# A two-layer network behind an attention scan: the 399 parts of the first block written in another order

## The chip, the cores and the metric

One core of one Trainium2 chip runs the kernel. The metric is the device time in microseconds (us) from the first to the last instruction of one execution, as the median of several executions. The chip's engines are named as the profile names them: PE (TensorE, matrix products; PEld is its weight load), DVE (VectorE), ACT (ScalarE), POOL (GpSimd) and SP (SyncE, which here only issues DMAs). Each engine runs its own list of instructions strictly in the order in which it is written, and waits at an instruction until the semaphores that it needs have come.

## The reference

```python
def _attn_ref(r, k, v, w, u):              # B=4, H=8, S=768, D=48
    for t in range(S):
        cur = np.einsum('bhd,bhe->bhde', u[None] * kt, vt)
        y[:, :, t] = np.einsum('bhd,bhde->bhe', rt, state + cur)
        state = wt[:, :, :, None] * state + np.einsum('bhd,bhe->bhde', kt, vt)

def _moe_ref(x, w1, w2, w3, w_out):        # 3072 tokens, 384 -> 1024 -> 1024 -> 384
    h = ((x @ w1) * (x @ w2)) @ w3
    return h @ w_out

def _moe2_ref(x, w_in, w_out):             # 384 -> 2048 -> 384
    h = x @ w_in
    return (h - np.tanh(h)) @ w_out
```

The output of the attention is the input x of the first network, whose output is the input of the second. The weights of the networks come as 64-bit floats.

## The kernel before

The sequence is cut into 24 **chunks** of 128 positions, and the tokens into six **blocks** of 512, which is four chunks each. The first network can start on a block when the attention of its four chunks is done. w3 and w_out are multiplied into one matrix W first (the **folds**), since nothing stands between them.

The change touches the first block only. There everything has to be prepared for the first time, and it is written out by hand as a list, `ORDER`, of 399 short names; each name is a part of the work and a number. The list is carried out as it stands, and each engine gets its instructions in the order in which the parts give them. The names that matter:

- **Attention of chunk n.** `LPn`, `LKn` load its five tensors (SP). `Dan`, `Dbn` are two scans on DVE, `Drn` a small step on POOL between them, `Dkn` and `Dcn` element-wise products (DVE for chunks 0 to 3, POOL from chunk 4). On PE stand `Sdn` (a diagonal term, chunks 0 to 3; tile psd), `San` (scores, tile psA), `Stn` (transposes, psk), `Sun` (state update, psu), `On` (outputs, psy) and `Wn` (for the first four chunks: a small product that puts 16 rows in their place, psy again). ACT copies out of PSUM (`Sen`, `Sbn`, `SBn`, `Skn`, `Vn`, `Xn`), POOL masks (`Smn`, `SMn`), DVE ends with `Tn` (state) and `Yn` (the rest of x).
- **Weights.** Each piece of 64-bit weights goes through four parts: `lw` fetches it into one of three buffers named st (SP, line 146), `wa` and `wb` take it apart (ACT, lines 168 and 174), and `wj` joins the halves (DVE, two passes, lines 178 and 180). The letter behind says which weight: `a` for the first layer (w1 and w2 together, eight pieces of 768 columns), `o` for w_out (four pieces of 768), `x` and `y` for the two halves of w3 (eight of each, 512 columns). A first-layer piece is then rounded (`wha`, ACT) and its rest taken (`wsa`, DVE, line 202).
- **Fold f** (`Ff`, PE, line 486, tile psW): 8 products of 128x384 that need all of w_out and both halves f of w3. `Faf` (ACT) and `Fdf` (DVE, line 202) write W.
- **First network, piece f of 8.** `Pf` is the product with w1 and w2 (PE, 18 matmuls, tiles psa and psb, lines 206 to 208), `Gaf`, `Gmf`, `Gbf`, `Gsf` the gate (ACT, DVE, ACT, DVE), `Qf` the product with W (PE, 9 matmuls, tile acc). All of `P` needs x of the four chunks.

The three buffers st are reused in turn, so a fetch waits until the piece three places before it has been joined on DVE. SP, too, works in order: a load behind a waiting fetch waits with it. Chunks 4 to 7, which belong to the next block, are prepared inside the list as well, between the products.

After the list the kernel goes on with `pair` (line 780 on), two pieces of the first network and one chunk at a time, and then with the second network. None of that is touched.

Of the kernel before, what the change touches and what calls it, by code (L numbers as in the profile page):

```python
# [40 lines left out]


ORDER = """
LP0 LK0 lwa3 lwa1 lwa2 Da0 LP1 Dr0 K0 Db0 LK1 Dk0 Sd0 Dc0 waa3 wba3 Sa0 Se0 wja3 waa1 Sf0 wba1 St0 lwy3 Sb0 wja1 Sk0
Sm0 SB0 Su0 waa2 SM0 Da1 lwa0 wha3 O0 T0 Dr1 wba2 U0 Db1 LP2 wha1 LK2 V0 Dk1 W0 wsa3 Sd1 X0 Dc1 way3 Se1 wby3 Sf1 Y0
Sa1 wsa1 St1 SB1 Da2 Sb1 SM1 Sk1 wja2 Sm1 waa0 Su1 Dr2 O1 T1 wba0 lwo0 Dk2 U1 Db2 wha2 LP3 Sd2 V1 LK3 wsa2 W1 Se2 Dc2
Sf2 X1 wao0 Y1 Sa2 wja0 St2 Sb2 SB2 Sm2 Da3 lwo1 Sk2 SM2 wbo0 Su2 Dk3 Dr3 wha0 O2 T2 Db3 U2 LP4 wsa0 Sd3 V2 LK4 Dc3
wao1 W2 Se3 X2 wjo0 Sa3 Sf3 SB3 Da4 lwo2 Sb3 St3 SM3 wbo1 Y2 Sm3 Sk3 wjy3 Dr4 O3 Db4 lwo3 wao2 wjo1 Dc4 Su3 LK5 LN4 V3
wbo2 W3 T3 X3 lwa4 wjo2 wao3 U3 Sa4 LP5 wbo3 Y3 lwy0 P0 Sb4 wjo3 SB4 Sm4 Dt4 lwx0 SM4 waa4 De4 St4 LN5 P1 C4 Ga0 Sk4
wba4 Da5 way0 wby0 wja4 Dr5 O4 wax0 Ga1 Dt5 Db5 lwa5 wbx0 Su4 LK6 X4 P2 V4 wha4 T4 Dc5 Gm0 wsa4 Gb0 wjx0 waa5 U4 W4  # L50
lwx2 Sa5 LP6 wjy0 Ga2 wba5 P3 Gm2 lwy2 Sb5 wja5 Gb2 Sm5 SB5 wax2 SM5 Gs2 lwx3 wha5 Y4 wbx2 F0 Da6 Ga3 De5 Dr6 Gm3 LN6
Db6 Gb3 Gs3 Dc6 wsa5 P4 Fa0 Gm1 way2 Fd0 Gb1 Dt6 wjx2 wby2 wax3 Gs1 lwa6 wbx3 wjy2 Sa6 Ga4 P5 wjx3 lwy4 Sb6 SB6 Sm6
De6 lwx1 SM6 Gm4 LN7 waa6 C5 Gb4 F3 wba6 C6 Ga5 Gs4 Dt7 wja6 Gm5 wha6 lwx4 St6 Gs0 F2 Fa3 wsa6 wax1 Sk6 Fd3 wbx1 way4
wjx1 wby4 lwy1 wjy4 Su6 Fa2 O5 wax4 lwx5 Fd2 wbx4 wjx4 Q0 way1 LP7 LK7 V5 X5 T6 lwa7 W5 wby1 U6 Y5 F4 Gb5 wjy1 Gs5
lwx7 LP8 Da7 De7 Dr7 Db7 LN8 F1 Fa4 wax5 Fd4 Dc7 waa7 wbx5 wax7 wjx5 wba7 Da8 lwy6 wbx7 Sa7 Dt8 Fa1 wja7 O6 Sb7 SB7
St7 LK8 V6 Sm7 Fd1 X6 lwy7 Sk7 wjx7 Q1 SM7 way6 Dr8 W6 wha7 lwy5 C7 P6 wby6 wsa7 Y6 wjy6 way7 wby7 Q2 De8 lwx6 Ga6
wjy7 LN9 Su7 Gm6 F7 T7 Gb6 Db8 U7 LP9 Gs6 Dc8 O7 Fa7 way5 Fd7 wax6 Q3 LK9 wby5 X7 wjy5 wbx6 P7 V7 wjx6 W7 Y7 Z7 Q4 Ga7
Gm7 Gb7 F5 Gs7 F6 Fa5 Fd5 Q5 Fa6 Fd6 Q6 Q7
""".split()


# [978 lines left out]
```

## Time and profile before

| what | value |
|---|---|
| median of 3 runs | 907.2 us (905.99 to 907.22) |
| the profiled execution, its own time | 908.82 us |
| its span, first to last instruction | 907.1 us |
| mean granted PE clock | 0.982 |
| PE busy in the span | 861.9 us (95%) |
| DVE, ACT, POOL busy | 614.3, 483.0, 227.3 us |
| DMA | 93.31 MB, mean 103 GB/s |

The profile says for each instruction when it ran and what ended the idle time of its engine before it. The time of the profiled execution lies 1.7 us over its span, and 1.6 us over the median of the three runs. The granted clock is the share of full speed that PE was given: its two levels are 1.2 and 2.4 GHz, shown as 0.5 and 1.0.

### The profile page before, as it was taken

How to read it: one execution, taken by the hardware profiler on the slowest of the kernel's cores; microseconds unless marked ns; L12 is line 12 of the kernel's file. 1: busy time of each engine (PE TensorE's matmuls, PEld its weight loads, DVE VectorE, ACT ScalarE, POOL GpSimd, SP SyncE). 2: the span in 40 equal slices, each digit the busy share in tenths (PEclk: the TensorE clock that was granted, in tenths of full speed). 3: DMA queues.
4: the chain of work that ended last, by engine and by line, in shares of the span. 5: the costliest groups of instructions: out<-in, count | busy, mean ns of one | idle time of the engine just before them, and what ended most of it. 6: DMA issues, size and time to landing. Idle time of an engine off the chain costs nothing.

```text
span 907.1 us, 12892 instructions
## 1 busy us (share of the span) xinstructions
PE 861.9 (95%) x4762; PEld 690.8 (76%) x4762; DVE 614.3 (68%) x884; ACT 483.0 (53%) x879; POOL 227.3 (25%) x223
## 2 busy tenths in 40 slices
PE   5879999999999999799999899999999999999996
PEld 4766767778777777577888688888888888888885
DVE  6889884365666666665567977667667577586763
ACT  4546652123223224422467766596696786786662
POOL 4356241053344543435226310010010010000000
PEclk9789999999999999899999999999999999999999
DMA  8586574134443364631253020220220310300001
GB/s 287 196 273 201 168 262 129 47 111 129 116 154 109 96 242 134 215 117 53 54 180 134 21 61 1 68 72 0 71 69 1 94 47 1 106 23 0 36 1 38
DMA packets 51623, 93.31 MB, mean 103 GB/s; under 512 B 5152, under 2 KB 22688, under 8 KB 51552
## 3 DMA queue, kind: packets, MB, share of 16 engines
q1 hardware_dynamic: 51552, 92.41, 32.2%
q8 instruction: 39, 0.64, 0.3%
q14 instruction: 32, 0.26, 0.1%
HBM read 80.99 MB, written 9.44 MB: 100 GB/s over the span
## 4 chain that ended last, share of the span: by engine, by line
PE 49%; issue 3%; POOL 2%; DVE 1%; DMA 1%; ACT 1%; SPq 0%; ACTq 0%; POOLq 0%
PE acc L206 8%; PE acc L208 8%; PE acc L207 8%; PE psh L206 7%; PE psh L208 7%; PE psh L207 7%; POOL w L202 1%; DMA st<-w 1%; PE psa L206 1%; PE psa L207 1%; PE psa L208 1%; PE psb L207 1%; PE psb L206 1%; PE psb L208 1%; PE psy L395 0%
## 5 line engine op out<-in xcount | busy, mean ns | idle before, releaser
L516 DVE TENSOR_TENSOR g<-psh,g 128x512 fp32r<-128x512 f32 (+1 forms) x99 | 66.4, 672 | 55.3 <-ACT g L515 55.0
L206 PE MATMUL psh<-xt,w 128*128 128x512 f32 x252 | 98.1, 389 | 0.5 <-DVE g L516 0.5
L208 PE MATMUL psh<-xt,w 128*128 128x512 f32 x252 | 98.0, 389 | 0.0
L207 PE MATMUL psh<-xt,w 128*128 128x512 f32 x252 | 98.0, 389 | 0.0
L206 PE MATMUL acc<-g,w 128*128 128x512 f32 x252 | 98.0, 389 | 0.0
L207 PE MATMUL acc<-g,w 128*128 128x512 f32 x252 | 98.0, 389 | 0.0
L208 PE MATMUL acc<-g,w 128*128 128x512 f32 x252 | 98.0, 389 | 0.0
L515 ACT CAST g<-psh 128x512 fp32r<-128x512 f32 (+1 forms) x99 | 56.3, 570 | 63.0 <-DVE psh L582 63.0
L512 POOL TENSOR_TENSOR xt<-x2l,xt 128x512 fp32r<-128x512 f32 x18 | 24.4, 1366 | 258.4 <-ACT xt L511 258.3
L580 DVE TENSOR_TENSOR psh<-psh,z 128x512 f32<-128x512 f32 (+1 forms) x99 | 67.2, 679 | 27.0 <-ACT z L577 26.7
L581 DVE SCALAR_TENSOR_TENSOR psh<-s,psh 128x512 f32<-128x512 f32 (+1 forms) x99 | 67.1, 678 | 19.0 <-ACT s L578 12.6
L577 ACT ACTIVATE z<-psh 128x512 f32<-128x512 f32 (+1 forms) x99 | 57.6, 582 | 30.9 <-PE psh L208 29.3
L582 DVE SCALAR_TENSOR_TENSOR psh<-s,psh 128x512 f32<-128x512 f32 (+1 forms) x99 | 67.2, 679 | 9.5
L578 ACT ACTIVATE s<-z,qa 128x512 f32<-128x512 f32 (+1 forms) x99 | 70.5, 712 | 2.4
L579 ACT ACTIVATE s<-z,qa 128x512 f32<-128x512 f32 (+1 forms) x99 | 69.0, 697 | 0.0
L515 ACT CAST g<-psb 128x512 fp32r<-128x512 f32 x40 | 23.4, 585 | 84.9 <-DVE psb L843 48.8
L206 PE MATMUL psa<-xt,w 128*128 128x512 f32 x144 | 61.8, 429 | 6.9 <-DMA xt<-y 3.3
L337 POOL TENSOR_SCALAR_AFFINE_SELECT A<-A 128x512 f32<-128x512 f32 x48 | 37.6, 804 | 90.9 <-ACT A L332 90.7
L206 PE MATMUL psb<-xt,w 128*128 128x512 f32 x144 | 56.9, 395 | 2.5 <-ACT a L531 2.2
L208 PE MATMUL acc<-g,W 128*128 128x512 f32 x144 | 56.3, 391 | 2.2 <-DVE W L202 2.2
L206 PE MATMUL acc<-g,W 128*128 128x512 f32 x144 | 57.8, 401 | 0.0
L207 PE MATMUL psa<-xt,w 128*128 128x512 f32 x144 | 57.6, 400 | 0.0
(141 smaller groups left out, 1984.0 us busy)
## 6 DMA issues: line engine op xcount, KB each, us to landing
st<-w SPq DMA_DIRECT2D x24, 768.0 KB, 4.4
st<-w3F SPq DMA_DIRECT2D x16, 512.0 KB, 4.7
P<-wP SPq DMA_DIRECT2D x24, 258.0 KB, 2.8
ws<-wS SPq DMA_DIRECT2D x24, 256.0 KB, 3.4
kd<-kT SPq DMA_DIRECT2D x24, 256.0 KB, 3.8
rd<-rT SPq DMA_DIRECT2D x24, 256.0 KB, 4.0
vn<-vN SPq DMA_DIRECT2D x24, 256.0 KB, 3.6
wb<-wP SPq DMA_DIRECT2D x24, 256.0 KB, 3.4
```

Source lines behind the costliest of these rows:

```text
L206: nc.tensor.matmul(ps, lhs(0), rhs(1), start=start, stop=False)
L207: nc.tensor.matmul(ps, lhs(0), rhs(0), start=False, stop=False)
L208: nc.tensor.matmul(ps, lhs(1), rhs(0), start=False, stop=stop)
L337: nc.gpsimd.affine_select(out=A, in_=A, pattern=[[0, NP], [1, C]], compare_op=ALU.is_gt, fill=0.0, base=0, channel_multiplier=-1)
L515: nc.scalar.copy(t[:, 0, :], x)
L516: nc.vector.tensor_sub(t[:, 1, :], x, t[:, 0, :].bitcast(F32))
L577: nc.scalar.activation(out=z, in_=p, func=AF.Square)
L578: nc.scalar.activation(out=s1, in_=z, func=AF.Square, scale=QS, bias=qa[:, 0:1])
L579: nc.scalar.activation(out=s2, in_=z, func=AF.Square, scale=QS, bias=qa[:, 1:2])
L580: nc.vector.tensor_mul(p, p, z)
L581: nc.vector.scalar_tensor_tensor(out=p, in0=s1, scalar=QB1, in1=p, op0=ALU.add, op1=ALU.mult)
L582: nc.vector.scalar_tensor_tensor(out=p, in0=s2, scalar=QB2, in1=p, op0=ALU.add, op1=ALU.mult)
```

## The change

The same 399 parts stand in another order. Three things move. All four pieces of w_out and the halves of w3 are fetched and joined from the start, where three first-layer pieces stood. Folds 0 to 4 stand among the parts of chunks 2 and 3 and fold 5 behind the scores of chunk 4, all ahead of the first product P0; before, fold 0 stood behind four of the products and folds 5 and 6 near the end of the list. The first-layer pieces 0 to 7 are fetched and joined behind that, in the order of their use. No part is added or left out. The first two and the last two lines of the list, before and after:

```diff
-LP0 LK0 lwa3 lwa1 lwa2 Da0 LP1 Dr0 K0 Db0 LK1 Dk0 Sd0 Dc0 waa3 wba3 Sa0 Se0 wja3 waa1 Sf0 wba1 St0 lwy3 Sb0 wja1 Sk0
-Sm0 SB0 Su0 waa2 SM0 Da1 lwa0 wha3 O0 T0 Dr1 wba2 U0 Db1 LP2 wha1 LK2 V0 Dk1 W0 wsa3 Sd1 X0 Dc1 way3 Se1 wby3 Sf1 Y0
...
-wjy7 LN9 Su7 Gm6 F7 T7 Gb6 Db8 U7 LP9 Gs6 Dc8 O7 Fa7 way5 Fd7 wax6 Q3 LK9 wby5 X7 wjy5 wbx6 P7 V7 wjx6 W7 Y7 Z7 Q4 Ga7
-Gm7 Gb7 F5 Gs7 F6 Fa5 Fd5 Q5 Fa6 Fd6 Q6 Q7
+LP0 LK0 lwo0 lwo1 lwx0 Da0 LP1 Dr0 K0 Db0 LK1 Dk0 Sd0 Dc0 wao0 wbo0 Sa0 Se0 wjo0 wao1 Sf0 wbo1 St0 wax0 wjo1 lwy0 Sb0
+SB0 Sm0 Sk0 wbx0 SM0 Su0 Da1 lwo2 O0 Dk1 Dr1 T0 way0 Db1 U0 LP2 wby0 wjx0 Sd1 wao2 LK2 V0 Dc1 lwo3 Se1 W0 wbo2 Sf1
...
+Y6 SB7 Sm7 wsa7 Gb5 St7 SM7 Q3 Gs5 Sk7 Da8 Su7 C7 Dr8 P6 T7 Db8 U7 LP9 De8 Dc8 LN9 O7 Ga6 Gm6 Gb6 Q4 LK9 V7 Gs6 X7 W7
+Y7 P7 Z7 Q5 Ga7 Gm7 Gb7 Q6 Gs7 Q7
```

On PE, from the diagonal term and the placing (`Sd2`, `W1`) at the end of chunk 1's work to the transposes of chunk 2. A w with a number is a half of w3, so two rows of psW are one fold:

```order
 L309 MATMUL psd<-ub,rk 128x2 x4
 L414 MATMUL psy<-y_148 128x128 x3
+L486 MATMUL psW<-wo,w_202 128x384 x4
+L486 MATMUL psW<-wo,w_254 128x384 x4
+L486 MATMUL psW<-wo,w_378 128x384 x4
+L486 MATMUL psW<-wo,w_400 128x384 x4
 L327 MATMUL psA<-rd,kd 128x128 x8
+L486 MATMUL psW<-wo,w_452 128x384 x4
+L486 MATMUL psW<-wo,w_444 128x384 x4
 L349 MATMUL psk<-ident,kd 128x128 x4
-L362 MATMUL psu<-vn,ks 64x48 x8
```

Two folds now stand ahead of chunk 2's scores (psA) and one between its scores and its transposes; the state update (psu) has gone behind the outputs.

On DVE, from the last piece of w_out to the first rest of a fold, after the change (cm into wo is a join of w_out, cm into w_ a join of a half of w3, W the rest of fold 0):

```order
L178 SCALAR_TENSOR_TENSOR cm<-cm,cl 128x768
L180 SCALAR_TENSOR_TENSOR wo<-st,cm 128x768
L289 RECIPROCAL ends<-R 128x64
L292 SCALAR_TENSOR_TENSOR ws<-ws,ends 128x512
L434 TENSOR_TENSOR xt<-psy,xt 128x3x128
L178 SCALAR_TENSOR_TENSOR cm<-cm,cl 128x512
L180 SCALAR_TENSOR_TENSOR w_378<-st,cm 128x512
L178 SCALAR_TENSOR_TENSOR cm<-cm,cl 128x512
L180 SCALAR_TENSOR_TENSOR w_400<-st,cm 128x512
L302 TENSOR_TENSOR rd<-rd,P 128x512
L303 TENSOR_TENSOR kd<-kd,ws 128x512
L202 TENSOR_TENSOR W<-psW,W 128x384
```

Before, the same stretch of chunk 2 held a first-layer piece instead:

```order
L289 RECIPROCAL ends<-R 128x64
L292 SCALAR_TENSOR_TENSOR ws<-ws,ends 128x512
L202 TENSOR_TENSOR w_2_367<-cm,w_2_367 128x768
L302 TENSOR_TENSOR rd<-rd,P 128x512
L303 TENSOR_TENSOR kd<-kd,ws 128x512
L434 TENSOR_TENSOR xt<-psy,xt 128x3x128
L178 SCALAR_TENSOR_TENSOR cm<-cm,cl 128x768
L180 SCALAR_TENSOR_TENSOR cm<-st,cm 128x768
```

So the products rd and kd, which chunk 2's scores need, now stand behind the two halves for fold 1.

On ACT, around `V0`, the copy of 16 rows of chunk 0's output (y_148), first before and then after the change:

```order
L199 CAST w_3_228<-cm 128x768
L174 ACTIVATE cl<-st,qa 128x768
L199 CAST w_1_258<-cm 128x768
L409 COPY y_148<-psy 128x128
L430 CAST xt<-psy 128x3x128
```

```order
L174 ACTIVATE cl<-st,qa 128x512
L168 ACTIVATE cm,tops<-st 128x512
L174 ACTIVATE cl<-st,qa 128x512
L168 ACTIVATE cm,tops<-st 128x768
L409 COPY y_148<-psy 128x128
```

The copy now stands behind the first step (cm) of a piece of 768 columns, the third of w_out, whose fetch must have landed.

## Rows read from the trace of the kernel before

**Rows 1.** The page: PE's busy time in the span; its granted clock in 40 slices

```profile
PE 861.9 (95%) x4762; PEld 690.8 (76%) x4762; DVE 614.3 (68%) x884; ACT 483.0 (53%) x879; POOL 227.3 (25%) x223
...
PEclk9789999999999999899999999999999999999999
```

**Rows 2.** Windows: stretch, length, busy time of each engine, PE's clock, DMA

```profile
8.58:36.28 27.70, 23.44 (x189) 20.54 (x189) 22.01 (x26) 16.48 (x31) 10.16 (x13) 0.82 0.78 269
36.28:89.14 52.86, 43.66 (x362) 35.04 (x361) 47.47 (x55) 29.20 (x56) 30.32 (x28) 0.90 0.69 229
89.14:174.90 85.76, 83.51 (x433) 57.95 (x432) 53.98 (x79) 36.03 (x76) 21.05 (x19) 1.00 0.48 151
```

**Rows 3.** Waits of PE from 36.28 to 89.14 us, longest first

```profile
PE psk L349 <- DVE xt L434: 3.4, 1, 3.4
```

**Rows 4.** Windows of 2 us, PE alone: length, busy time, clock, DMA

```profile
50.00:52.00 2.00, 1.35 (x8) 0.50 0.77 310
52.00:54.00 2.00, 2.00 (x20) 0.50 0.57 144
54.00:56.00 2.00, 2.00 (x38) 0.86 0.96 386
...
78.00:80.00 2.00, 2.00 (x14) 0.61 0.43 121
80.00:82.00 2.00, 2.00 (x7) 0.54 0.89 291
```

**Rows 5.** Groups of PE from 89.14 to 174.9 us by shape: count, busy, mean ns, idle

```profile
L208 PE MATMUL acc<-g,W 128*128 128x512 f32 x24 | 9.5, 396 | 2.2 <-DVE W L202 2.2
```

**Rows 6.** Timeline of PE: start, duration; chunk 1's scores, chunk 2, a fold

```profile
24.14 2.50 PE L327 MATMUL psA<-rd,kd 48*128 48x128 f32 x16 [1.06 <-issue]
...
35.44 0.91 PE L414 MATMUL psy<-y 128*128 128x128 f32 x6
36.28 1.16 PE L327 MATMUL psA<-rd,kd 48*128 48x128 f32 x16
...
39.27 0.67 PE L362 MATMUL psu<-vn,ks 128*64 128x48 f32 x16 [1.11 <-ACT ks L354]
...
43.70 0.91 PE L414 MATMUL psy<-y 128*128 128x128 f32 x6
...
98.93 5.32 PE L486 MATMUL psW<-wo,w 128*128 128x384 f32 x16
104.08 0.60 PE L349 MATMUL psk<-ident,kd 128*128 128x128 f32 x4
```

**Rows 7.** Groups of DVE from 0 to 175 us by shape: count, busy, mean ns

```profile
L178 DVE SCALAR_TENSOR_TENSOR cm<-cm,cl 128x512 int32<-128x512 int32 x16 | 12.8, 801 | 6.4 <-ACT cl L174 6.4
L178 DVE SCALAR_TENSOR_TENSOR cm<-cm,cl 128x768 int32<-128x768 int32 x12 | 12.8, 1063 | 3.2 <-ACT cd L312 2.9 <-ACT cl L174 0.2
L292 DVE TENSOR_TENSOR_SCAN ws<-ws,ends 128x512 f32<-128x512 f32 x9 | 12.6, 1399 | 0.3
L180 DVE SCALAR_TENSOR_TENSOR w<-st,cm 128x512 int32<-128x512 int32 x16 | 12.3, 768 | 1.1
...
L180 DVE SCALAR_TENSOR_TENSOR cm<-st,cm 128x768 int32<-128x768 int32 x8 | 10.1, 1266 | 0.3
L202 DVE TENSOR_TENSOR w<-cm,w 128x768 fp32r<-128x768 f32 x8 | 8.7, 1086 | 0.0
```

**Rows 8.** Timeline of DVE: the last product of chunk 2; one pass of a join

```profile
33.56 0.69 DVE L303 TENSOR_TENSOR kd<-kd,ws 128x512 f32<-128x512 f32 x1
...
74.52 1.67 DVE L178 SCALAR_TENSOR_TENSOR cm<-cm,cl 128x512 int32<-128x512 int32 x1
```

**Rows 9.** DMA issues up to 100 us: count, size, median us from issue to landing

```profile
st<-w3F SPq DMA_DIRECT2D x8, 512.0 KB, 5.4
st<-wo SPq DMA_DIRECT2D x4, 768.0 KB, 4.4
```

**Rows 10.** Timeline of ACT: the copy of 16 rows of chunk 0's output

```profile
20.78 0.27 ACT L409 COPY y<-psy 128x128 f32<-128x128 f32 x1 [1.55 <-PE psy L401]
```

More of the change, by code (lines that the diff above doesn't have):

```diff
@@ L43 @@
 ORDER = """
-LP0 LK0 lwa3 lwa1 lwa2 Da0 LP1 Dr0 K0 Db0 LK1 Dk0 Sd0 Dc0 waa3 wba3 Sa0 Se0 wja3 waa1 Sf0 wba1 St0 lwy3 Sb0 wja1 Sk0
-Sm0 SB0 Su0 waa2 SM0 Da1 lwa0 wha3 O0 T0 Dr1 wba2 U0 Db1 LP2 wha1 LK2 V0 Dk1 W0 wsa3 Sd1 X0 Dc1 way3 Se1 wby3 Sf1 Y0
-Sa1 wsa1 St1 SB1 Da2 Sb1 SM1 Sk1 wja2 Sm1 waa0 Su1 Dr2 O1 T1 wba0 lwo0 Dk2 U1 Db2 wha2 LP3 Sd2 V1 LK3 wsa2 W1 Se2 Dc2
-Sf2 X1 wao0 Y1 Sa2 wja0 St2 Sb2 SB2 Sm2 Da3 lwo1 Sk2 SM2 wbo0 Su2 Dk3 Dr3 wha0 O2 T2 Db3 U2 LP4 wsa0 Sd3 V2 LK4 Dc3
-wao1 W2 Se3 X2 wjo0 Sa3 Sf3 SB3 Da4 lwo2 Sb3 St3 SM3 wbo1 Y2 Sm3 Sk3 wjy3 Dr4 O3 Db4 lwo3 wao2 wjo1 Dc4 Su3 LK5 LN4 V3
@@ L49 @@
[L49 to L53, printed above, removed]
@@ L54 @@
-wjx1 wby4 lwy1 wjy4 Su6 Fa2 O5 wax4 lwx5 Fd2 wbx4 wjx4 Q0 way1 LP7 LK7 V5 X5 T6 lwa7 W5 wby1 U6 Y5 F4 Gb5 wjy1 Gs5
-lwx7 LP8 Da7 De7 Dr7 Db7 LN8 F1 Fa4 wax5 Fd4 Dc7 waa7 wbx5 wax7 wjx5 wba7 Da8 lwy6 wbx7 Sa7 Dt8 Fa1 wja7 O6 Sb7 SB7
-St7 LK8 V6 Sm7 Fd1 X6 lwy7 Sk7 wjx7 Q1 SM7 way6 Dr8 W6 wha7 lwy5 C7 P6 wby6 wsa7 Y6 wjy6 way7 wby7 Q2 De8 lwx6 Ga6
-wjy7 LN9 Su7 Gm6 F7 T7 Gb6 Db8 U7 LP9 Gs6 Dc8 O7 Fa7 way5 Fd7 wax6 Q3 LK9 wby5 X7 wjy5 wbx6 P7 V7 wjx6 W7 Y7 Z7 Q4 Ga7
-Gm7 Gb7 F5 Gs7 F6 Fa5 Fd5 Q5 Fa6 Fd6 Q6 Q7
+LP0 LK0 lwo0 lwo1 lwx0 Da0 LP1 Dr0 K0 Db0 LK1 Dk0 Sd0 Dc0 wao0 wbo0 Sa0 Se0 wjo0 wao1 Sf0 wbo1 St0 wax0 wjo1 lwy0 Sb0
@@ new lines @@
+SB0 Sm0 Sk0 wbx0 SM0 Su0 Da1 lwo2 O0 Dk1 Dr1 T0 way0 Db1 U0 LP2 wby0 wjx0 Sd1 wao2 LK2 V0 Dc1 lwo3 Se1 W0 wbo2 Sf1
+wjy0 X0 Sa1 Sb1 Y0 lwx1 SB1 wjo2 St1 Sm1 Sk1 SM1 Su1 O1 wao3 T1 lwy1 Da2 U1 LP3 wbo3 Dk2 Dr2 wax1 wjo3 Sd2 LK3 V1 wbx1
+W1 way1 X1 Db2 F0 lwy2 wby1 Se2 Sf2 Y1 wjx1 wjy1 lwx2 Fa0 Dc2 F1 lwx3 way2 Fd0 wby2 Dk3 wax2 wjy2 wbx2 wjx2 lwy3 Sa2
+Fa1 Da3 lwx4 wax3 F2 Sb2 Fd1 Dr3 SB2 Sm2 Db3 wbx3 SM2 way3 wjx3 wby3 wjy3 lwy4 St2 wax4 O2 Sk2 Dc3 lwa0 wbx4 Fa2 wjx4
+way4 Su2 LK4 V2 Fd2 lwx5 Sd3 wby4 T2 U2 W2 wjy4 Se3 waa0 Sf3 Sa3 LP4 X2 lwy5 F3 Sb3 Y2 SB3 Sm3 wba0 SM3 wja0 Da4 wha0
@@ new lines @@
+lwa1 St3 Fa3 O3 wsa0 Dr4 Sk3 wax5 Fd3 way5 Db4 wbx5 Su3 LN4 LK5 V3 F4 wby5 T3 Dc4 wjx5 waa1 wjy5 wba1 lwx6 U3 wja1
+lwy6 Dt4 LP5 W3 Fa4 Sa4 X3 Fd4 lwx7 wha1 Y3 F5 De4 wax6 wsa1 LN5 Sb4 SB4 Sm4 wbx6 SM4 Da5 way6 wby6 wjx6 Dr5 St4 Fa5
+Dt5 P0 C4 wax7 lwy7 Sk4 wbx7 wjy6 Fd5 lwa2 wjx7 way7 Su4 Ga0 O4 wby7 T4 lwa3 Gm0 U4 wjy7 Gb0 LP6 F6 V4 LK6 X4 waa2 Gs0
+lwa4 W4 Db5 wba2 waa3 Y4 Dc5 wba3 wja2 P1 Fa6 Fd6 wha2 lwa5 De5 wsa2 LN6 wja3 Sa5 Ga1 waa4 F7 Sb5 Gm1 lwa6 SB5 Sm5 Da6
+Gb1 wha3 SM5 Gs1 wba4 Dr6 wsa3 Dt6 waa5 C5 P2 waa6 wja4 Fa7 wba5 Fd7 wha4 lwa7 De6 O5 wba6 wsa4 LN7 Ga2 Db6 P3 V5 LP7
@@ L59 @@
+LK7 X5 W5 Dc6 Gm2 waa7 Y5 Gb2 wja5 P4 Ga3 Dt7 Gs2 wha5 Gm3 wba7 wsa5 Gb3 Da7 Sa6 Ga4 Gs3 Dr7 Q0 Gm4 Sb6 SB6 De7 Sm6
+Gb4 Db7 LN8 SM6 St6 Q1 Sk6 Gs4 Dc7 C6 Su6 P5 wja6 Dt8 T6 wha6 wja7 U6 O6 LP8 Ga5 Sa7 V6 LK8 wsa6 X6 wha7 Q2 W6 Gm5 Sb7
+Y6 SB7 Sm7 wsa7 Gb5 St7 SM7 Q3 Gs5 Sk7 Da8 Su7 C7 Dr8 P6 T7 Db8 U7 LP9 De8 Dc8 LN9 O7 Ga6 Gm6 Gb6 Q4 LK9 V7 Gs6 X7 W7
+Y7 P7 Z7 Q5 Ga7 Gm7 Gb7 Q6 Gs7 Q7
 """.split()
```

## The prediction

> **What bounds the kernel now.** I read the page first. PE is busy for 95% of the span, and its clock stands at 9 in nearly every slice; the slices below that lie in the first tenth [rows 1]. So time can be won only where PE idles or runs at half clock, and the change can reach only the first block, whose last product ends at 174.9 us. I therefore cut that block into stages. Up to 36.28 us (end of chunk 1 on PE) PE is busy 23.4 of 27.7 us at a mean clock of 0.82; from there to 89.14 us it is busy 43.7 of 52.9 us at 0.90; in the last 85.8 us it is busy 83.5 us at 1.00 [rows 2]. DVE is the other loaded engine: 47.5 us of the middle stage, but only 54.0 of 85.8 us in the last one [rows 2].
>
> The waits of PE in the middle stage tell why. The longest, 3.4 us, is for DVE, which was still joining weights while the transposes of chunk 3 stood at the head of PE's list [rows 3]. PE has nothing else to do there: each chunk's attention is a chain through five engines, and the first product needs x of all four chunks. In the last stage the only wait of size is 2.2 us, for the rest of a fold that stands late in the order [rows 5].
>
> What PE loses after 36.28 us, in three terms:
> - idle in the middle stage: 52.86 - 43.66 = 9.2 us [rows 2];
> - half clock: busy time times (1 - clock), over the five windows where the clock is clearly below 1: 0.68 + 1.00 + 0.28 + 0.78 + 0.92 = 3.7 us [rows 4]. The first three follow the idle of 3.4 us [rows 3];
> - idle in the last stage: 85.76 - 83.51 = 2.2 us [rows 2, 5].
>
> Together 15.1 us. That is the most that the change can win after 36.28 us, since no work is added or taken away.
>
> **What moves.** Six of the eight folds now stand ahead of P0. One fold takes 104.08 - 98.93 = 5.15 us on PE [rows 6], so 31 us of work that needs nothing from the attention is put into a stage that had 9.2 us idle. The order excerpt shows the place: F0 and F1 stand directly behind W1, so PE has work from 36.3 us on without a break, if the folds are fed. P0 comes much later than before, and that costs nothing by itself: the products and folds are all work of the same list, and only idle time counts.
>
> **Are the folds fed?** A fold needs joins on DVE, so I count DVE up to the last join of F0. Before, DVE finished kd of chunk 2 at 33.56 + 0.69 = 34.2 us [rows 8]. After, the same stretch holds four joins of w_out for three of the first layer (one more, 1.06 + 1.27 = 2.3 us), two joins of w3 (2 x 1.57 = 3.1 us) and none of three rests (3 x 1.09 = 3.3 us) [rows 7]; scan, reciprocal and two products of chunk 2 come later (1.4 [rows 7], twice 0.69 [rows 8], and about 0.5 as my estimate for the reciprocal: 3.3 us). So 34.2 + 2.3 + 3.1 - 3.3 - 3.3 = 33.0 us, and PE arrives at 35.44 + 0.84 = 36.28 us [rows 6]: 3 us to spare. F1: scan and reciprocal 1.9 us, then DVE waits for x of chunk 1 (W1 is done at 36.3, ready on DVE at about 37.3 after a copy and a subtraction of half a microsecond each, an estimate), then two joins of 3.1 us: 40.4 us. F0 ends at 36.3 + 5.2 = 41.5 us: 1 us to spare. F2: kd by 41.8, the rest of F0 at 42.5 (it waits for F0), one product 0.7, two joins 3.1: 46.3 us, against 36.3 + 10.4 + 1.2 = 47.9 us on PE: 1.6 us to spare. After that PE falls further behind DVE, since each chunk adds 7.2 us of attention to PE (36.28 to 44.61 less the wait of 1.11 [rows 6]) besides its folds.
>
> The fetches: three buffers st, 5.4 us from issue to landing for a half of w3 [rows 9]. With two steps on ACT and the join, a buffer comes round in about 5.4 + 1.4 + 1.6 = 8.4 us (the ACT share is an estimate), so a fold's two halves every 5.6 us. PE takes 31 us of folds and 16 us of attention from 36.3 us to P0, so a fold every 8 us. That is enough.
>
> The first-layer pieces now come behind the folds. P0 starts at about 36.3 + 31 + 16 = 83 us. DVE has then some 63 us of work left in the block: of 123.5 us busy between 8.58 and 174.9 us [rows 2] its new list has, counted with the means of rows like [rows 7], 60 us up to the rest of the second piece (an estimate). PE has about 79 us left, so the joins (2.3 us) and rests (1.1 us) of a piece lie beside products. Without that cover each late piece would cost up to 3.4 us.
>
> **What is added as waits.** V0 now stands behind a step on the third piece of w_out. Before it ran at 20.78 us [rows 10]. That fetch can be issued when the second join frees its buffer (about 18 us) and lands 4.4 us later [rows 9], so V0 runs at about 23.3 us. Behind it on ACT wait W0's copy and the scores' copies, on PE W0 and Sa1. Sa1 started only at 24.14 us, after a wait of 1.06 [rows 6], so I charge 0.4 us. Two more changes between fold and product on PE cost a few tenths: 0.3 us. And PE will not be gapless: its best long stage before still lost 2.25 of 85.76 us, 2.6% [rows 2], so I charge 2.6% of the 124 us from 36.3 us to the end of the block, 3.2 us.
>
> **Sum.** 15.1 - 0.4 - 0.3 - 3.2 = 11.2 us. The profiled execution took 908.8 us, 1.7 more than its span, so it would take 897.6; it lies 1.6 us over the median of the runs shown, which gives 896.0 us for the median. The first block then ends near 164 us.
>
> **A rule that speaks against it.** One pass of a join of a half of w3 took 1.67 us at 74.5 us [rows 8], while the mean of such passes is 0.77 to 0.80 [rows 7]. The Trainium skill (SBUF — State Buffer, section "Who interferes with whom") says that a DVE instruction with two SBUF inputs and a GpSimd instruction that reads SBUF exclude each other, and the later one blocks for the whole instruction. The long pass agrees with such a block. By the mean the sum stands as above; with every join at the blocked price it is the second rival below.
>
> **Rivals.**
> - *Half of it comes.* Folds F1 and F2 have 1 to 1.6 us to spare by sums of means. If joins slip by 2 to 3 us, PE idles at each, with the clock falling after it as it did behind the 3.4 us wait [rows 3, 4]: two or three times 1 to 2 us. The time is 898.5 to 902. Nothing in the rows excludes it. 0.2.
> - *Slower: the joins meet POOL.* Ten joins of w3 now lie in the stage in which POOL masks and multiplies for chunks 1 to 4 (30.3 us busy before [rows 2]). At 1.67 [rows 8] instead of 0.78 [rows 7] a pass, 20 passes cost DVE 18 us more. It starts with 1 to 2 us to spare, so PE would wait some 16 us and the attention behind the folds with it: 5 us slower, 912. It decides from about 0.65 us more per pass. Against it: the means [rows 7] contain the blocked passes already. 0.08.
> - *No change.* PE's idle time comes back later: pieces 2 to 7 of the first layer arrive late because DVE, in order, waits at each gate for its product and joins the next piece only then. Six pieces at 1.9 us would use up the gain: 906 to 908. DVE's 63 us in PE's 79 us speak against it. 0.08.
> - *More.* The new order loses next to nothing: 15.1 us won, 892 us. 0.04.
>
> The forecast itself, 893.5 to 898.5 us, gets 0.6. A measurement of this kernel tells about 0.2% (1.8 us) from no change. The range reaches from 893 to 902.5 us, the forecast with the first rival, so that about 0.2 is left outside. Faster: 0.6 + 0.2 + 0.04 = 0.84; within 0.2%: 0.08; slower: 0.08.
>
> **What would show it.** In the changed kernel's profile: folds in a row from about 36.5 us; PE busy over 50 of the 52.9 us from 36.3 to 89.1 us, at a clock near 1.0; no wait of PE for a join or a rest (lines 178 to 202) over 1 us; P0 at about 83 us; the last acc product of the block near 164 us; and the time behind it as before. It is wrong if psW products wait for DVE (first rival, or the second if the joins take 1.6 us a pass), or if psa products wait for the rest of a first-layer piece (third).

## The result, and the profile after

The changed kernel took 897.26 us (median of six runs, 896.06 to 901.52); the kernel before took 907.21 us on the same chip (six runs, 905.99 to 912.52). The ratio is 0.9889, with a 95% interval of 0.9859 to 0.9920: 10.1 us faster (7.3 to 12.8). 11.2 us were predicted. The profiled execution of after took 896.06 us, with a span of 894.4 us; it was the fastest of its six.

The page of after, PE's row and its granted clock, beside [rows 1]:

```profile
PE 857.5 (96%) x4762; PEld 686.8 (77%) x4762; DVE 619.8 (69%) x884; ACT 483.7 (54%) x879; POOL 223.1 (25%) x223
...
PEclk9999999999999999899999999999999999999999
```

The windows of after by stage; the first two stretches are those of [rows 2], the third ends at 164 us, where the prediction put the end of the first block:

```profile
8.58:36.28 27.70, 20.63 (x190) 18.17 (x191) 21.92 (x28) 17.56 (x36) 10.57 (x13) 0.94 0.81 281
36.28:89.14 52.86, 52.86 (x373) 36.79 (x372) 46.99 (x59) 31.98 (x68) 17.75 (x19) 1.00 0.68 235
89.14:164.00 74.86, 73.31 (x431) 55.32 (x430) 61.31 (x78) 33.87 (x62) 29.24 (x27) 1.00 0.52 173
```

In the middle stage PE is busy all of the 52.86 us, at a clock of 1.00, where it was busy 43.66 us at 0.90. From 36.28 to 170 us PE waits twice, 1.6 us together:

```profile
PE psA L327 <- DVE Sb L368: 0.9, 1, 0.9
PE psk L349 <- DVE xt L434: 0.7, 1, 0.7
```

The timeline of PE in after, at the place of [rows 6], shows what fills the stage: two folds in one run behind the placing of chunk 1's 16 rows (line 414), a third behind the scores of chunk 2, and so on up to the first product (line 206):

```profile
35.12 0.91 PE L414 MATMUL psy<-y 128*128 128x128 f32 x6
35.87 10.49 PE L486 MATMUL psW<-wo,w 128*128 128x384 f32 x32
46.29 1.16 PE L327 MATMUL psA<-rd,kd 48*128 48x128 f32 x16
47.38 5.43 PE L486 MATMUL psW<-wo,w 128*128 128x384 f32 x16
...
75.67 5.43 PE L486 MATMUL psW<-wo,w 128*128 128x384 f32 x16
80.94 0.60 PE L349 MATMUL psk<-ident,kd 128*128 128x128 f32 x4
81.29 0.48 PE L206 MATMUL psa<-xt,w 128*128 128x512 f32 x1
```

The last product of the first block ended at 160.1 us (175.0 before). A place that both orders pass in the same way lies a little later, the scores of chunk 9. In the timeline of PE before, and then after:

```profile
186.67 1.16 PE L327 MATMUL psA<-rd,kd 48*128 48x128 f32 x16 [1.03 <-POOL kd L303]
```

```profile
173.23 1.16 PE L327 MATMUL psA<-rd,kd 48*128 48x128 f32 x16 [1.00 <-POOL kd L303]
```

The lead there is 13.4 us; the spans differ by 12.7. From these scores to the end of the span all the profiled kernels, those of the experiments too, took between 719 and 722 us: 720.4 before and 721.2 after. So the whole gain lies ahead of this place.

### The profile page after: what moved, and what is told of

It reads as the page before. It is cut to its first block, busy times and chain, and to the rows that moved or that the text cites. A ratio compares the mean times of both kernels' runs of the same rounds, so it can differ in the third digit from the quotient of the medians.

```text
span 894.4 us, 12900 instructions
## 1 busy us (share of the span) xinstructions
PE 857.5 (96%) x4762; PEld 686.8 (77%) x4762; DVE 619.8 (69%) x884; ACT 483.7 (54%) x879; POOL 223.1 (25%) x223
## 4 chain that ended last, share of the span: by engine, by line
PE 50%; issue 3%; POOL 2%; DVE 2%; DMA 1%; ACT 1%; SPq 0%; ACTq 0%; POOLq 0%
PE acc L206 8%; PE acc L208 8%; PE acc L207 8%; PE psh L206 7%; PE psh L208 7%; PE psh L207 7%; POOL w L202 1%; DMA st<-w 1%; PE psa L206 1%; PE psa L208 1%; PE psa L207 1%; PE psb L206 1%; PE psb L208 1%; PE psb L207 1%; PE psy L395 0%
## 5 line engine op out<-in xcount | busy, mean ns | idle before, releaser
L581 DVE SCALAR_TENSOR_TENSOR psh<-s,psh 128x512 f32<-128x512 f32 (+1 forms) x99 | 67.1, 678 | 19.1 <-ACT s L578 12.7
L206 PE MATMUL psa<-xt,w 128*128 128x512 f32 x144 | 61.8, 429 | 4.9 <-DMA xt<-y 3.0
L206 PE MATMUL psb<-xt,w 128*128 128x512 f32 x144 | 57.5, 399 | 2.7 <-ACT a L531 2.7
L206 PE MATMUL acc<-g,W 128*128 128x512 f32 x144 | 58.1, 404 | 0.0
L208 PE MATMUL psa<-xt,w 128*128 128x512 f32 x144 | 57.7, 401 | 0.0
L207 PE MATMUL psa<-xt,w 128*128 128x512 f32 x144 | 57.5, 399 | 0.0
L207 PE MATMUL psb<-xt,w 128*128 128x512 f32 x144 | 56.9, 395 | 0.0
```

Source lines behind the costliest of these rows:

```text
L206: nc.tensor.matmul(ps, lhs(0), rhs(1), start=start, stop=False)
L207: nc.tensor.matmul(ps, lhs(0), rhs(0), start=False, stop=False)
L208: nc.tensor.matmul(ps, lhs(1), rhs(0), start=False, stop=stop)
L581: nc.vector.scalar_tensor_tensor(out=p, in0=s1, scalar=QB1, in1=p, op0=ALU.add, op1=ALU.mult)
```

## The experiments

**Is it the folds ahead of P0?** Two kernels take the folds back behind P0, six of them or three, and leave the joins where after has them. (`late` names the folds moved; they read the two halves of fold 6, so the work is the same, but W is not the reference's.)

```diff
-W1 way1 X1 Db2 F0 lwy2 wby1 Se2 Sf2 Y1 wjx1 wjy1 lwx2 Fa0 Dc2 F1 lwx3 way2 Fd0
+W1 way1 X1 Db2 lwy2 wby1 Se2 Sf2 Y1 wjx1 wjy1 lwx2 Dc2 lwx3 way2
...
-wja2 P1 Fa6 Fd6
+wja2 P1 F3 Fa6 Fa2 Fd6 Fd2
...
+        h = 6 if f in late else f
-                psW[f][:, :DM], w3t[f][m // (NF // 2)]
+                psW[f][:, :DM], w3t[h][m // (NF // 2)]
```

> The changed order, but folds 0 to 5 (with their roundings and rests) moved from chunks 2 to 4 to behind the product P0, between the products; all joins stay where they are. Folds 0 to 5 read the two halves of w3 that belong to fold 6, since there are only four buffers for them, so W is not the reference's. Theory (the folds fill PE's idle time in the chunk stage): from 36 us to P0 PE idles again, over 10 us in sum, partly at half clock; P0 comes at 70 to 74 us instead of 81, but 31 us of folds stand behind it; the last acc product of the block at 180 to 184 us instead of 160; 915 to 921 us. Rival (the gain comes from the new order of the joins on DVE and ACT, the first-layer pieces last, and not from where the folds stand): 896 to 900 us.

Measured: 924.71 us (922.39 to 927.14), ratio 1.0171 (1.0125 to 1.0216), slower than before by more than the change had won. Its windows, its longest waits of PE, and its first product:

```profile
36.28:89.14 52.86, 34.03 (x247) 28.12 (x247) 42.27 (x52) 29.08 (x62) 18.68 (x19) 0.68 0.67 224
```

```profile
PE psk L349 <- DVE xt L434: 8.4, 2, 5.4
PE psA L327 <- issue: 5.8, 1, 5.8
```

```profile
79.91 0.78 PE L206 MATMUL psa<-xt,w 128*128 128x512 f32 x1
```

> As the run before, but only folds 3, 4 and 5 moved behind P0 (they read the halves of fold 6); folds 0 to 2 stay in chunk 2. Theory: PE stays busy to about 58 us, then chunk 3 is a bare chain again; P0 at 70 to 72 us; PE idle of 4 to 6 us and 1 to 2 us of half clock come back: 902 to 905 us. Rival: 896 to 900 us.

Measured: 911.87 us (908.92 to 914.32), ratio 1.0032 (1.0007 to 1.0057).

```profile
36.28:89.14 52.86, 42.93 (x340) 32.35 (x338) 45.79 (x55) 31.12 (x68) 18.87 (x19) 0.87 0.71 232
```

```profile
80.51 0.78 PE L206 MATMUL psa<-xt,w 128*128 128x512 f32 x1
```

The theory holds, and both came out slower than I expected, for one reason. I had let P0 come 7 to 11 us earlier once PE is rid of the folds. It came at 79.9 and 80.5 us instead of 81.3: with the joins of six folds ahead of it on DVE, x of chunk 3 is not ready sooner. So six folds, 31 us of work on PE, put P0 off by only 1.4 us. Counted from the placing of chunk 1's 16 rows, which starts at 35.1 us in after, 36.6 with six and 37.7 with three folds moved back, P0 follows after 46.2, 43.3 and 42.8 us, which makes it about 3 us. Each fold behind P0 costs its full time. From P0 to the last product of the block after takes 160.1 - 81.3 = 78.8 us. With 5.2 us for each fold moved back, 79.9 + 78.8 + 31.2 = 189.9 us and 80.5 + 78.8 + 15.6 = 174.9 us; measured 189.1 and 174.3.

**The wait of 2.2 us in the last stage [rows 5], alone.** In before, the rest of fold 1 is set directly behind its rounding:

```diff
-Dt8 Fa1 wja7 O6 Sb7 SB7 St7 LK8 V6 Sm7 Fd1 X6
+Dt8 Fa1 Fd1 wja7 O6 Sb7 SB7 St7 LK8 V6 Sm7 X6
```

> The order before the change with one part moved: the rest of fold 1 (Fd1, DVE) directly behind its rounding, ahead of the join of the last first-layer piece. Theory (third term of the sum: the acc product of Q1 waits 2.2 us for that rest): the wait is gone and the time is 2 us less, 904.5 to 905.5. Rival (PE waits for something else right behind it): no change.

Measured: 905.91 us (903.14 to 908.73) against 909.48 us of before on that chip, ratio 0.9962 (0.9939 to 0.9985), 3.4 us faster (1.4 to 5.5). The window of its last stage has no idle time left:

```profile
89.14:174.90 85.76, 85.76 (x460) 60.07 (x460) 57.24 (x82) 36.42 (x75) 20.02 (x19) 1.00 0.49 160
```

From the start of the first product on acc to the start of the last one of the block it took 59.6 us instead of 62.2, 2.6 us less. This term of the sum stands by itself, and one move of one name wins it.

**How much room do the folds have?** In after, one product of chunk 3 on DVE, ahead of fold 2's joins, is made seven times (lines behind it move down by one):

```diff
-        nc.vector.tensor_mul(t["rk"], t["r"], t["k"])
+        for _ in range(7 if n == 3 else 1):
+            nc.vector.tensor_mul(t["rk"], t["r"], t["k"])
```

> The kernel after, with the product of r and k of chunk 3 on VectorE (behind the first rest of fold 0, ahead of the two joins that feed fold 2) made seven times over instead of once, which leaves its values as they are: six more instructions of 0.60 us, 3.6 us. Theory (a fold can start only when its weights are joined, and TensorE has no other wait left in this stage): the joins of fold 2 ended at 46.3 us, 1.1 us before fold 2 started, so about 2.5 us of the 3.6 come out as a wait of TensorE ahead of fold 2; TensorE's busy time in 36.28 to 89.14 falls from 52.9 to about 50.4, P0 moves from 81.3 to about 83.8, and the whole takes 2.5 us longer than the kernel after (899.0 to 900.5 where that has 897.3). Rival (VectorE, with 47 of these 52.9 us busy, takes the 3.6 us up in its idle time before TensorE needs it): no wait above 0.5 us, and the time of the kernel after within 0.7 us.

Measured: 901.94 us (899.88 to 902.82), ratio 0.9921 (0.9894 to 0.9948): 7.2 us faster than before (4.7 to 9.6), where after wins 10.1. These two intervals overlap, so the places in the profile decide. Fold 2 in its timeline of PE:

```profile
53.31 7.12 PE L487 MATMUL psW<-wo,w 128*128 128x384 f32 x16 [2.63 <-DVE w L180]
```

The wait came out as 2.6 us where 2.5 were expected, in part by luck: the six extra products took 4.4 us and not 3.6, and the room ahead of fold 2 was 1.7 us in this execution and not 1.1. What I had not counted is the clock: fold 2 took 7.12 us instead of 5.43, with a granted clock of 0.50 from 55 to 57 us. The late join cost its delay and 1.7 us of half clock behind it: from the start of fold 0 to P0 it is 49.8 us instead of 45.4.

**V0 behind the third piece of w_out.** It ran at 25.19 us, not at 23.3. The timeline of ACT in after, beside [rows 10], shows the step ahead of it waiting for the fetch:

```profile
24.29 0.90 ACT L168 ACTIVATE cm<-st 128x768 f32<-128x768 f32 x1 [2.86 <-DMA st<-wo]
...
25.19 0.25 ACT L409 COPY y<-psy 128x128 f32<-128x128 f32 x1
```

In the next kernel the two steps on that piece stand behind the scores of chunk 1:

```diff
-wby0 wjx0 Sd1 wao2 LK2 V0 Dc1 lwo3 Se1 W0 wbo2 Sf1 wjy0 X0 Sa1 Sb1
+wby0 wjx0 Sd1 LK2 V0 Dc1 lwo3 Se1 W0 Sf1 wjy0 X0 Sa1 wao2 wbo2 Sb1
```

> The changed order with the two ACT steps on the third piece of w_out (wao2, wbo2) moved from ahead of V0 to behind Sa1, so that the copy of chunk 0's 16 rows no longer waits for that fetch. Theory: V0 at 21 to 22 instead of 25.2 us, chunk 1's scores 2 to 3 us earlier; F0 needs the last join of w_out, which ended at 35.7 us, so at most 1.5 us comes through: 895.5 to 897.3. Rival (every us of chunk 1 counts on PE): 894.5.

Measured: 897.61 us (895.87 to 898.97), ratio 0.9871 (0.9839 to 0.9903); no difference from after. V0 ran at 22.44 us, and PE's wait of 1.95 us was gone, but the next one took its place: 1.97 us ahead of the scores of chunk 1, which need kd from DVE (the profile names no releaser there; kd ended at 26.04 us and the scores started at 26.14). The outputs of chunk 1 then took 5.18 us at half clock, and fold 0 started at 37.74 us. So neither the theory nor the rival came true.

**The same kernel again.** That the outputs had taken 2.99 us in the profile of after, and 5.18 to 5.58 in those of its variants, made me doubt the first profile, so I profiled after twice more.

> The kernel after, unchanged, for a second profile of it. In its first profile TensorE's clock was back at full at 30 us and fold 0 started at 35.87 us. In the profiles of two kernels with the same order up to fold 0 (seven products instead of one; two moves behind P0) the outputs of chunk 1 took 5.58 us instead of 2.99 and fold 0 started at 39.10 and 38.78 us. Theory (the first profile caught the better of two courses, and the other is the usual one): fold 0 starts at 38.3 to 39.3 us, and the span is 2 to 3 us above 894.4. Rival (the two edits had something to do with it): fold 0 starts within 0.5 us of 35.87.

> The kernel after once more, for a third profile; expected as for the second: fold 0 at 38.3 to 39.3 us and a span of 896.5 to 897.5 by the theory, 35.9 and 894.4 by the rival.

Measured, one execution each: 898.78 and 899.31 us, spans 897.1 and 897.6; fold 0 at 38.27 and 37.70 us. That is near the theory's ranges, the third profile a little outside both, and far from the rival. The windows of 2 us of the first profile of after, then of the third:

```profile
26.00:28.00 2.00, 2.00 (x15) 1.78 (x16) 1.67 (x2) 0.88 (x2) 0.70 (x1) 0.50 0.94 360
28.00:30.00 2.00, 1.65 (x14) 1.18 (x12) 1.96 (x3) 0.93 (x2) 0.27 (x1) 0.74 0.87 266
30.00:32.00 2.00, 1.31 (x29) 1.26 (x31) 0.59 (x2) 2.00 (x5) 1.23 (x3) 1.00 0.61 162
32.00:34.00 2.00, 2.00 (x39) 1.83 (x36) 2.00 (x3) 1.10 (x3) 1.83 (x2) 1.00 0.46 168
```

```profile
26.00:28.00 2.00, 2.00 (x15) 1.77 (x16) 0.56 (x3) 0.69 (x2) 0.95 (x1) 0.50 0.85 348
28.00:30.00 2.00, 2.00 (x14) 1.37 (x12) 1.88 (x3) 1.01 (x2) 0.36 (x1) 0.50 0.76 300
30.00:32.00 2.00, 1.32 (x20) 1.24 (x22) 0.18 (x1) 2.00 (x5) 0.99 (x2) 0.50 0.45 127
32.00:34.00 2.00, 2.00 (x20) 1.67 (x18) 2.00 (x3) 1.04 (x3) 1.66 (x2) 0.50 0.38 150
```

The order is the same; in the first profile the clock is back at 30 us, in the third not until 34 to 36. The record names the chip of the second and third profile only, so whether the chip or the single execution decides is open. The first profile flattered the change by 1 to 3 us. In the second and third the scores of chunk 9 start at 175.5 and 175.3 us, a lead of 11.3 us.

**Does the idle time cost the clock?** Useless products (the identity by a constant, into a free tile) fill the wait ahead of W0 in after, seven or four of them:

```diff
+    def filler(_):
+        ps = big.tile([128, TB], F32, tag="big", name="psf")
+        for _ in range(4):
+            nc.tensor.matmul(ps[:, :DM], ident, fl(e0)[:, :DM], start=True, stop=True)
...
-wby0 wjx0 Sd1 wao2 LK2 V0
+wby0 wjx0 Sd1 H0 wao2 LK2 V0
```

> The kernel after, with seven products of the identity and a constant (128 x 384, float32, into a free tile that nobody reads; about 2.4 us at full clock) on TensorE between the diagonal of chunk 1 and the placing of the last channels of chunk 0, where it waited 1.95 us for ScalarE (V0, queued behind the third piece of w_out). Theory (the half clock from 26 us on follows that wait, and in this stage TensorE sets the end): the clock stays at full, the outputs of chunk 1 take about 3.0 us instead of 5.58, fold 0 starts at 35.9 to 36.5 us in every profile, and the whole is 2 to 3 us faster than the usual course of the kernel after, median 894.5 to 896. Rival (the clock falls for another reason, or the wait is not what it follows): the outputs still take 5.2 to 5.6 us, fold 0 starts at 38.5 to 39.5 us, and the time is that of the kernel after or up to 0.5 us more.

Measured: 897.75 us (894.96 to 900.94), ratio 0.9872 (0.9847 to 0.9897). The products took 0.68 us each, twice what I had counted (each shows as two instructions, and I had counted one), and ended 2 us too late. Even so the outputs of chunk 1 took 2.99 us, and fold 0 started at 36.47 us. The clock followed the theory; the time did not show it.

> The kernel after with four of the products at the place of the seven (a product took 0.68 us there and not the 0.34 that I had counted, so the seven overran the wait by more than 2 us and still fold 0 started at 36.47 us, with the outputs of chunk 1 at 2.99). Four take 2.7 us and end about when V0 does. Theory (the clock stays at full when the wait is filled, and then the last w_out join on VectorE, which ended at 35.73 us in the first profile of after, is the last thing that fold 0 waits for): the outputs of chunk 1 take 3.0 us, fold 0 starts at 35.7 to 36.3 us, 2 to 3 us ahead of the usual course of after (37.7 and 38.3 in its second and third profile), and the whole is 1.5 to 3 us faster than that, median 894.5 to 896.5. Rival (the seven held the clock by their length, not by closing the wait): the outputs take over 4 us again and the time is that of the kernel after.

Measured: 894.03 us (893.62 to 895.98), ratio 0.9846 (0.9822 to 0.9870): 14.0 us faster than before (11.8 to 16.2), the fastest kernel here, with 2.83 us of work that nobody reads. Its interval of the ratio just overlaps that of after (0.9859 to 0.9920); the places are clearer: it starts the scores of chunk 9 at 170.6 us, where the three profiles of after have 173.2, 175.5 and 175.3. The clock is on record for every run too: its mean is 0.991 to 0.993 in these five runs, 0.989 to 0.993 in the six with seven products, 0.984 to 0.991 in the eight of after. Two of its windows of 2 us, beside the same of after above:

```profile
26.00:28.00 2.00, 1.59 (x20) 1.16 (x18) 1.99 (x3) 1.39 (x4) 0.49 (x2) 1.00 0.88 317
...
30.00:32.00 2.00, 2.00 (x38) 1.75 (x34) 1.77 (x3) 2.00 (x4) 1.81 (x2) 1.00 0.82 277
```

Its timeline of PE, then that of the third profile of after:

```profile
22.34 2.83 PE L732 MATMUL psf<-e,ident 128*128 128x384 f32 x8
25.01 0.83 PE L414 MATMUL psy<-y 128*128 128x128 f32 x6
25.77 1.16 PE L327 MATMUL psA<-rd,kd 48*128 48x128 f32 x16
...
29.18 1.09 PE L389 MATMUL psy<-rd,Sb 48*64 48x128 f32 x16
...
33.76 10.49 PE L486 MATMUL psW<-wo,w 128*128 128x384 f32 x32
```

```profile
25.30 1.65 PE L414 MATMUL psy<-y 128*128 128x128 f32 x6 [2.56 <-ACT y L409]
26.88 2.08 PE L327 MATMUL psA<-rd,kd 48*128 48x128 f32 x16
...
31.70 1.97 PE L389 MATMUL psy<-rd,Sb 48*64 48x128 f32 x16
...
37.70 10.49 PE L486 MATMUL psW<-wo,w 128*128 128x384 f32 x32
```

W0 (line 414) starts at nearly the same time in both. It and the two attention rows shown behind it take about half as long, and fold 0 starts 3.9 us earlier. It even starts 2 us earlier than I had expected: I had the last join of w_out, at 35.73 us, as its bound. DVE reached that join earlier too (it ended at 33.91 us), because DVE no longer waited for the state of chunk 1, and fold 0 started 0.15 us ahead of its end, since that piece is read by the last quarter of a fold.

**The half clock in the middle stage, alone.** The same products in before, five or three, fill its wait of 3.40 us ahead of the transposes of chunk 3:

```diff
-lwo2 Sb3 St3 SM3
+lwo2 Sb3 H3 St3 SM3
```

> The kernel before, with five products of the identity and a constant (128 x 384, float32, into a free tile that nobody reads) on TensorE between the scores and the transposes of chunk 3, where it waited 3.40 us for VectorE. Nothing else is moved, so the idle time is filled with work of no use and only the clock can change. By my sum (half clock counts by itself): the granted clock of 50 to 56 us rises from half to full, O3 takes about 3.0 us instead of 4.32, P0 starts 1 to 1.5 us earlier, and the whole is 1 to 2 us faster than the kernel before. Rival (the start of P0 is set by VectorE's list, which ends the last rest of x at 59.96 us whatever TensorE does): O3 is shorter, but P0 starts at 60.0 as before, with a longer wait ahead of it, and the time is that of the kernel before within 0.7 us.

Measured: 907.36 us (904.13 to 911.78), ratio 0.9984 (0.9963 to 1.0006). The outputs of chunk 3 (O3) took 2.99 us instead of 4.32, but started later; P0 started 19.82 us behind O2 instead of 20.15.

> The kernel before with three of the same products, instead of five, between the scores and the transposes of chunk 3 (the five took 5.2 us at half clock and overran the wait of 3.4 us by 1.5 us). By my sum (half clock counts by itself): the transposes start when they did before, O3 takes 3.0 to 3.5 us instead of 4.32, P0 starts about 1 us earlier against O2 (18.8 to 19.2 us behind its start instead of 20.15), and the whole is about 1 us faster. Rival (VectorE's list sets the start of P0: its last rest of x follows the last pass of a w_out join with no idle time): O3 is shorter by 1 us, the wait ahead of P0 grows by as much (from 1.56 to about 2.5 us), P0 starts within 0.3 us of 20.15 us behind O2, and the time is that of the kernel before.

Measured: 906.48 us (903.53 to 909.33), ratio 0.9965 (0.9947 to 0.9983). Again O3 took 2.99 us and P0 started 19.82 us behind O2, 0.33 us sooner than before. The timeline of DVE says why; its last rest of x (line 434) follows a join with no idle time:

```profile
58.93 1.15 DVE L180 SCALAR_TENSOR_TENSOR wo<-st,cm 128x768 int32<-128x768 int32 x1
60.01 0.55 DVE L434 TENSOR_TENSOR xt<-psy,xt 128x384 fp32r<-128x384 f32 x1
```

By the places the rival is right: in before, DVE set the start of P0, and the half clock ahead of it was hidden. That the wait ahead of P0 would grow was wrong (1.36 us), since the scores of chunk 4 came later. The runs say 3.2 us faster (1.5 to 4.8), which these places don't explain. The one profile is of the slowest of the ten runs (909.33 us, span 907.6), and in it the half clock came back elsewhere: behind the wait ahead of P0 the granted clock is 0.50 from 60 to 66 us, where before has 1.00, and from P0 to the scores of chunk 9 it took 128.1 us instead of 126.7. The nine faster runs may have been spared that, but no profile of one is kept, so it stays open.

**The two waits that are left.** In after, the state of chunk 6 ahead of the join of piece 6, and the rest of piece 6 behind the last rest of chunk 6:

```diff
-P5 wja6 Dt8 T6 wha6 wja7 U6 O6 LP8 Ga5 Sa7 V6 LK8 wsa6 X6 wha7 Q2 W6 Gm5 Sb7 Y6 SB7
+P5 T6 U6 wja6 Dt8 wha6 wja7 O6 LP8 Ga5 Sa7 V6 LK8 X6 wha7 Q2 W6 Gm5 Sb7 Y6 wsa6 SB7
```

> The kernel after, with two small moves in the part behind P0: on VectorE the state of chunk 6 ahead of the join of first-layer part 6 instead of behind it, and the rest of first-layer part 6 behind the last rest of chunk 6 instead of ahead of it. Those are the two places at which TensorE still waited between 36 and 170 us (0.9 us for the state ahead of the scores of chunk 7, 0.7 us for x ahead of its transposes). Theory (TensorE is the bound of this stretch, so each of its waits counts in full): both waits go, the last product of the block's second layer ends about 1.5 us earlier (158.6 instead of 160.1), and the whole is 1.0 to 1.8 us faster than the kernel after (895.5 to 896.3 where that has 897.3). Rival (the products that wait for the later rest, P6 first, take the idle time over): waits of the same sum at other instructions, and the time of the kernel after.

Measured: 896.45 us (895.74 to 898.56), ratio 0.9865 (0.9837 to 0.9892); not to be told from after. Its waits of PE from 36 to 170 us:

```profile
PE psk L349 <- DVE xt L434: 1.1, 1, 1.1
PE acc L206 <- ACT a L531: 1.1, 1, 1.1
```

The rival was right: one wait went, one grew, and one came, 2.2 us in sum. From the start of fold 0 to the scores of chunk 9 it takes 137.5 us, as in after (137.4).

## Why the prediction was right, step by step

**Idle time of the middle stage, 9.2 us: right.** PE is busy there without a break. The folds behind P0 again gave all of it back and more.

**Half clock, 3.7 us: right as a sum, in part not as a cause of its own.** The clock is 1.00 there after. But while DVE's list set the start of P0, the 1.3 us that O3 lost were hidden: without them P0 came 0.33 us sooner. By these places that part (2.0 of the 3.7 us, ahead of P0) is won only together with the idle time, by an order in which PE sets the pace; then it counts, as the 1.7 us behind the late join showed. The time of the kernel with three products, 3.2 us under before, does not fit this and is open. The other 1.7 us (78 to 82 us, behind P0) no run tested alone.

**Idle time of the last stage, 2.2 us: right**, 2.6 us when taken alone.

**The feeding of the folds: the ends nearly right, one cause missed.** In after, the last joins ahead of folds 0, 1 and 2 end here on DVE's timeline:

```profile
34.77 0.96 DVE L180 SCALAR_TENSOR_TENSOR wo<-st,cm 128x768 int32<-128x768 int32 x1
...
40.36 0.69 DVE L180 SCALAR_TENSOR_TENSOR w<-st,cm 128x512 int32<-128x512 int32 x1
...
45.63 0.69 DVE L180 SCALAR_TENSOR_TENSOR w<-st,cm 128x512 int32<-128x512 int32 x1
```

That is 35.7, 41.1 and 46.3 us, against 33.0, 40.4 and 46.3 in the sum. The first is 2.7 us late. I added DVE's busy times without a change in its gaps, but the join stands in DVE's order behind the state of chunk 1, for which DVE waited 1.41 us (0.45 before), and the first join of all started at 13.7 us instead of 12.7; together that is about 1.9 of the 2.7 us. By the start of a fold, as I counted, the room was 0.1 us for fold 0 and for fold 1, not 3 and 1, and 1.1 for fold 2, not 1.6. For the first two the count was too strict: fold 0 reads the last piece of w_out in its last quarter, and fold 1 reads the half that was joined last in its second half.

**V0, 0.4 us: too small.** This is the term that was mis-sized. V0 came 4.4 us later than before and not 2.5, since the fetch of the third piece was issued at 18.6 us and took 5.7 us to land, where I had about 18 and 4.4. Over the six profiles with after's order up to there fold 0 starts at 38.0 us on average (35.87 to 39.10), over four of before's order the same place is passed at 37.0 (36.28 to 37.86): about 1.1 us instead of 0.4. The half clock behind V0's wait is no part of that difference: before had it too, with 5.21 us for the outputs of chunk 1. It lies ahead of 36.28 us, where the sum counted nothing to be won; filling the wait ahead of W0 won it.

**Idle time left over, 3.2 us: too large**, 1.6 us. With 1.1 for V0 the sum is 15.1 - 1.1 - 0.3 - 1.6 = 12.1 us, inside the interval of 7.3 to 12.8; the two errors partly cancelled. The 0.3 us for two more changes is a term that no run measured, and the 2 us between 12.1 and the measured 10.1 are not told from the noise. P0 at 83 us and the block's end near 164 us were 81.3 and 160.1 us in the first profile, 83.1 and 162.2 in the third.

**The rivals.** *Half of it* did not come: the only wait of a fold in these profiles is that of fold 2, behind the seven products of chunk 3. In after the room was smaller than the sum had it, as above. *Joins meet POOL:* the groups of after from 0 to 160 us, beside the same in [rows 7]:

```profile
L178 DVE SCALAR_TENSOR_TENSOR cm<-cm,cl 128x512 int32<-128x512 int32 x16 | 14.7, 920 | 0.3 <-ACT cl L174 0.2
L180 DVE SCALAR_TENSOR_TENSOR w<-st,cm 128x512 int32<-128x512 int32 x16 | 14.3, 891 | 0.9
```

A pass rose from 801 to 920 ns and from 768 to 891, by 0.12 us; the rival needed 0.65. POOL was in fact less busy beside the joins than I had assumed, 17.8 us of the middle stage instead of 30.3. The means also mix stages: from 36 to 81 us the passes were long before already, 1048 and 1010 ns, and shorter after, 986 and 852; but three pairs lay there before and ten lie there after. The Trainium skill (SBUF — State Buffer, "Who interferes with whom") has a DVE instruction with two SBUF inputs contend with a GpSimd instruction that reads SBUF; longer passes in that stage agree with that, but no run here took POOL's work away, so the cause of the 0.12 us is argued, not shown. *No change* did not come: in after no product waits for a piece of the first layer. *More* (15.1 us) did not come either.

## What to carry to other kernels

Work that waits for nothing belongs where a chain of dependent steps leaves an engine idle, and it is nearly free there only until that chain would have been done: compare when the next product could start with and without it. When two terms (idle and half clock) lie behind the same other engine's list, one of them alone may win little. A sum of busy times to a deadline must also hold the waits inside that list, and one profile of a start-up stage is one draw: a second one is cheap.

## What the runs showed of the hardware that was not expected

- Products that nobody reads made the kernel after faster: with 2.83 us of them in a wait of PE the granted clock stood at 1.00 (2.4 GHz) from 20 to 38 us, and the scores and the state products that follow took 1.16 and 0.67 us instead of 2.08 and 1.10 at 0.50 (1.2 GHz). In before, where DVE set the start of P0, five or three such products brought P0 forward by only 0.33 us.
- The same instructions in the same order got the full clock back at 30 us in one execution of after and after 34 us in two others.
- The clock of a window can miss it. In the kernel with three folds back, the window says 1.00, and the outputs take what they took at 0.50:

```profile
32.00:34.00 2.00, 2.00 (x20) 1.67 (x18) 2.00 (x3) 0.61 (x2) 1.79 (x2) 1.00 0.31 121
```

```profile
31.26 1.97 PE L389 MATMUL psy<-rd,Sb 48*64 48x128 f32 x16
```
